# Pooled attention with a noisy top-2 mixture of experts: head sums on another engine, small loads and the first batch in another order

## The chip, the cores and the metric

The kernel runs on one NeuronCore of a Trainium2 chip. The metric is device time in microseconds (us) of one execution. The engines are named as the profile names them: PE (TensorE, matmuls; PEld its weight loads), DVE (VectorE), ACT (ScalarE), POOL (GpSimd), SP (SyncE, which here issues most DMAs). Each engine works through its own queue in order, and an engine that waits holds up everything behind it in that queue.

## What is computed

```
k_p = k.reshape(B, H, S/8, 8, D).mean(3);  v_p likewise      # B=8, H=8, S=576, D=64
scores = q @ k_p^T / sqrt(D);  attn = softmax(scores);  x = attn @ v_p   # x: 4608 tokens x 512
noisy = x @ w_gate + log1p(exp(x @ w_noise)) * noise          # 8 experts
top2, weights = softmax over the two largest of noisy
out = sum over the token's 2 experts of weight * (relu(x @ w1[e]) @ w2[e])   # 512 -> 1024 -> 512
```

## The kernel before, in words

**Attention.** The eight batches are taken as four pairs (`pr` 0 to 3). A pair has five units: two of 256 tokens for each batch and one ("R") that holds the last 64 tokens of both. A unit's tokens are worked on in chunks of 128, so a pair has 9 chunks (`ci` 0 to 8) and the whole attention 36. `k_prep` and `v_prep` add up groups of eight rows of k and v on DVE. `qtr` turns a unit's q on PE (tile `qp`) and ACT copies it out (`qT`). `qk` makes scores on PE (`s`), their maximum on DVE (`mx`) and the exponentials on ACT (`ex`). `et` turns these (`ep`, `eT`), and `av` multiplies them with the block matrix `vbd`. Besides v, `vbd` holds for each head the products of v with that head's rows of the gate and noise weights (`wrb`, multiplied in the step `vr`), so `av` gives the attention output `xr` and, for each of the 8 heads, that head's part of the 16 router logits: `lg`.

**Routing.** `route(pr, ...)` is a generator that runs once per pair. It adds the 8 heads' parts of `lg` (the head sums: for 8 chunks together adds over 128x512, 128x256 and 128x128 elements, then the same for the last chunk over 64, 32 and 16), computes the noisy logits and the two best experts (DVE, four steps on ACT), ranks the tokens by a running count on PE (`rk`, from the mask `mb`), and hands over 18 scatters per pair (`rec_dram`, one DMA each from POOL's queue). The scatters wait in the list `scq` and are issued a few at a time by `advance`, none where `quiet` is 0. Behind them stand, in the same queue, the load of the records of the first expert's rows and the gathers of those rows (`fetch`, tile `xg`).

```
for a, b in ((c0, c1 - 1), (c1 - 1, c1)):
    for h in (4, 2):
        nc.gpsimd.tensor_add(lg[:, a:b, :h], lg[:, a:b, :h], lg[:, a:b, h:2 * h])
    nc.gpsimd.tensor_add(L[:, a - c0:b - c0], lg[:, a:b, 0], lg[:, a:b, 1])
```

**Experts.** Each of the 8 experts takes its rows in three groups: `stage1` multiplies with w1 (8 blocks `f`, line 1016), ACT and DVE split the result into two parts (`hh`, `hl`), and `stage2` multiplies with w2 (lines 1093 and 1127). Expert 0's groups need rows that the four pairs bring in turn: tokens of pairs 0 and 1 for the first group, pair 2 for the second, pair 3 for the third. The last group of each expert (`joined`) comes in three widths; a branch on the expert's row count picks one. The counts are read into PE registers by `count(e)`, which a scheduler places. Pair 3's `rk` matmuls stand on PE behind the first 48 matmuls of `stage1` (4 of the 8 blocks of the first group).

**Order.** Within a priority order that a scheduler keeps, the program's own order decides; `issue_after(x)` holds an instruction behind x. At the start SP issues, in this order: k of batch 0 (three DMAs), q of batch 0 (two), `qr` (the last 64 tokens of q), v of batch 0 (three), and then in `mid_consts` four small DMAs that bring the gate and noise weights turned and doubled, in runs of 8 numbers:

```
for dup in range(2):
    for i, w in enumerate((moe_w_gate, moe_w_noise)):
        nc.sync.dma_start(wr[dup * 64:dup * 64 + 64, :, i * E:(i + 1) * E],
                          w.rearrange("(h d) e -> d h e", d=D))
```

After them POOL copies `wr` into `wrb` (six copies), and SP goes on with k, q, `qr` and v of batch 1.

Of the kernel before, what the change touches and what calls it, by code (L numbers as in the profile page):

```python
# [19 lines left out]
def kernel(  # L20
# [164 lines left out]

    def mid_consts():
        wr = cp.tile([P, H, 2 * E], F32, name="wr")
        for dup in range(2):
            for i, w in enumerate((moe_w_gate, moe_w_noise)):
                nc.sync.dma_start(wr[dup * 64:dup * 64 + 64, :, i * E:(i + 1) * E],  # L190
                                  w.rearrange("(h d) e -> d h e", d=D))
        nc.gpsimd.memset(wrb, 0.0)
        for n in range(NEB):
            rs = slice((n % 2) * 64, (n % 2) * 64 + 64)
            ns = len(HEADS[n])
            nc.gpsimd.tensor_copy(wrb[rs, SLOT0[n]:SLOT0[n] + ns, :],
                                  wr[rs, HEADS[n][0]:HEADS[n][0] + ns, :])

    KT, VT, QT, QR = {}, {}, {}, {}
    lastl, lasta = [None], [None]  # L200

# [77 lines left out]
    def v_prep(b):  # L279
        vt = VT[b]  # L280
        vs = ap_.tile([P, NEB, D], F32, tag="vs", name=f"vs{b}")
        VS[b] = vs
        if PV >> b & 1:
            halves(vt, b, BST, ((0, 3), (3, 6)), PV)
            yield
        yield from pooled(vs[:BST], vt, b, 0, NEB, BST, DV | PV)

# [46 lines left out]
    def qtr(u, half, hp=None):  # L334
# [7 lines left out]
        for i in range(4):  # L342
            if kind == "R":
                src = QR[pr][:, 2 * i:2 * i + 2]
            else:
                src = QT[b][:, half * 4 + i, 2 * jp:2 * jp + 2]
            nc.tensor.transpose(qp[:, i], src.rearrange("p a d -> p (a d)"), ident)  # L347
        with tc.high_priority(offset=HP if hp is None else hp):
            nc.scalar.copy(qT[:, half * 4:half * 4 + 4], qp)

    def qk(u, g):
# [19 lines left out]
        else:  # L371
            s = ps2.tile([P, 512], F32, tag="s", name=f"s{nm}", bufs=SB)
            rows = [(jj, h) for h in GRP[g] for jj in range(2)]
            for i, h in enumerate(GRP[g]):
                nc.tensor.matmul(s[:, i * 2 * G:(i + 1) * 2 * G], qT[:, h], kbd[b % 2][:, h],  # L375
                                 start=True, stop=True)
        n = len(rows)
        sv = s[:, :n * G].rearrange("p (r g) -> p r g", g=G)
        mx = ap_.tile([P, 6], F32, tag="mx", name=f"mx{nm}", bufs=4)
        nc.vector.tensor_reduce(out=mx[:, :n], in_=sv, axis=AX, op=OP.max, negate=True)  # L380
        for i, (jj, h) in enumerate(rows):
# [112 lines left out]
    def route(pr, c0, c1, lg, psum):  # L494
# [10 lines left out]
        L = t(NCH, 2 * E)  # L505
        for a, b in ((c0, c1 - 1), (c1 - 1, c1)):
            for h in (4, 2):
                nc.gpsimd.tensor_add(lg[:, a:b, :h], lg[:, a:b, :h], lg[:, a:b, h:2 * h])  # L508
            nc.gpsimd.tensor_add(L[:, a - c0:b - c0], lg[:, a:b, 0], lg[:, a:b, 1])
            if b < c1:  # L510
# [53 lines left out]
        mb = rp.tile([P, NCH + 1, E], BF16, tag="mb", name=f"mb{pr}_{c0}")  # L564
        nc.gpsimd.memset(mb[:, n:], 0.0)
        V.tensor_add(mb[:, :n], ms[0], ms[1])
# [245 lines left out]
    if WU:  # L812
        wu = ps2.tile([P, 512], F32, tag="s", name="wu", bufs=SB)
        for i in range(WU):
            nc.tensor.transpose(wu[:, i % 4 * P:(i % 4 + 1) * P], ident, ident)
    load_q(0)
    load_qr(0)
    load_v(0)
    block_tiles()
    mid_consts()  # L820
    drain(k_prep(0))
# [36 lines left out]
    qtr(units[0], 0)  # L858
    qtr(units[0], 1)
    for g in range(3):  # L860
        qk(units[0], g)
    if ST & 1:
        qtr(units[1], 0, H0)
        qtr(units[1], 1, H0)
    drain(v_prep(0))
    if ST & 2:
# [8 lines left out]
    for i, (ui, u, jj) in enumerate(chunks):  # L875
# [9 lines left out]
        eT = None  # L885
        quiet = 0 if ci == 0 or ci == NCH - 1 and pr < NP - 1 else 1

# [288 lines left out]
    for i, g in enumerate(groups):  # L1176
# [3 lines left out]
        if joined(g):  # L1180
            count(e)
        stage1(g, (lambda f: hook1(i, f)) if i < 2 else flush if i == len(groups) - 1 else None)
# [131 lines left out]
```

## Time and profile before

| | us |
|---|---|
| runs (3) | 1023.31, 1026.31, 1027.18; median 1026.31 |
| the profiled execution | 1026.68 |
| its span on the core | 1024.9 |
| lies around the span | 1.78 |
| PE busy (share of the span) | 989.9 (97%) |
| DVE, POOL, ACT busy | 546.1, 377.5, 343.8 |

Attention takes the first 190 us or so, the experts the rest. Times in the profile count from the span's start. "Idle before" is how long an engine stood still ahead of an instruction, with what ended the wait behind the arrow. PEclk is the granted share of TensorE's full clock; 1.00 is 2.4 GHz and 0.50 is 1.2 GHz.

### The profile page before, as it was taken

To read this page: it belongs to the slowest core of one execution; us is meant where nothing else is said; L and a number is where in the kernel's file an instruction comes from. 1 tells how busy PE (TensorE), PEld (TensorE's weight loads), DVE (VectorE), ACT (ScalarE), POOL (GpSimd) and SP (SyncE) were. 2 spreads that over 40 slices of the span, in tenths; PEclk is the share of its full clock that TensorE was granted. 3 is DMA by queue.
4 is the path that set the end of the run, shared out by engine and by line. 5 is a ranking of instruction groups with operands and counts; after the bars stand their busy time and mean duration, and the time that the engine had idled before them with its cause. 6 is when DMAs were issued, how large, how long until landed. Compare 5 with 4: busy or idle time off the path is not lost.

```text
span 1024.9 us, 16467 instructions
## 1 busy us (share of the span) xinstructions
PE 989.9 (97%) x5832; PEld 888.6 (87%) x5832; DVE 546.1 (53%) x1261; ACT 343.8 (34%) x857; POOL 377.5 (37%) x433
## 2 busy tenths in 40 slices
PE   7999997979999999999999999999999999999996
PEld 6898896869998888898988898989888988898995
DVE  5799886583344454644464446444644455356341
ACT  4787785451213212411142124211421232123120
POOL 3023574846300442145115421551154215422514
PEclk8999998989999999999999999999999999999998
DMA  9989883344607765676267736772678358744623
GB/s 252 250 250 273 227 263 112 115 146 98 208 15 218 215 180 148 199 238 206 74 188 219 239 114 201 249 217 70 182 235 256 93 161 256 245 144 135 211 87 136
DMA packets 136006, 187.61 MB, mean 183 GB/s; under 512 B 29123, under 2 KB 84052, under 8 KB 135898
## 3 DMA queue, kind: packets, MB, share of 16 engines
q1 hardware_dynamic: 110458, 119.09, 40.5%
q0 software_dynamic: 25440, 67.05, 21.0%
q8 instruction: 72, 1.18, 0.5%
q14 instruction: 36, 0.29, 0.1%
HBM read 123.31 MB, written 70.74 MB: 189 GB/s over the span
## 4 chain that ended last, share of the span: by engine, by line
PE 87%; POOL 3%; issue 3%; ACT 2%; DMA 2%; DVE 1%; SPq 1%; POOLq 0%; ACTq 0%; DVEq 0%
PE bank L1016 37%; PE bank L1127 28%; PE bank L1093 10%; PE a L408 4%; PE s L375 2%; PE ep L393 2%; POOL rec_dram L637 1%; PE qp L347 1%; DMA v<-in_v_dram 1%; ACT ex L382 1%; ACT eT L395 1%; POOL lg L508 1%; POOL out_dram L1072 1%; PE s L365 1%; DMA rec_dram<-rec,pos 0%
## 5 line engine op out<-in xcount | busy, mean ns | idle before, releaser
L1016 PE MATMUL bank<-xh,w 128*128 128x512 f32 (+6 forms) x1536 | 391.2, 339 | 0.0
L1016 PEld LDWEIGHTS bank<-xh,w 128*128 128x128 f32 x1536 | 271.1, 189 | 20.6
L1127 PE MATMUL bank<-w,hh 128*128 128x512 f32 x880 | 271.3, 389 | 0.0
L1016 PE MATMUL bank<-xl,w 128*128 128x512 f32 (+6 forms) x768 | 260.3, 339 | 0.0
L1027 ACT ACTIVATE hh<-bank 128x512 fp32r<-128x512 f32 (+4 forms) x192 | 97.3, 508 | 460.0 <-PE bank L1016 435.7
L1028 DVE SCALAR_TENSOR_TENSOR hl<-bank,hh 128x512 fp32r<-128x512 f32 (+4 forms) x192 | 111.0, 579 | 242.2 <-ACT hh L1027 242.2
L1127 PEld LDWEIGHTS bank<-w,hh 128*128 128x128 f32 x880 | 164.9, 188 | 33.8
L1127 PE MATMUL bank<-w,hl 128*128 128x512 f32 x440 | 171.4, 389 | 0.0
L1016 PEld LDWEIGHTS bank<-xl,w 128*128 128x128 f32 x768 | 145.0, 189 | 10.4
L1064 DVE SCALAR_TENSOR_TENSOR pv<-bank,raw,pv 128x128 f32<-128x128 f32 x196 | 55.5, 342 | 109.1 <-PE bank L1127 62.4
L1068 POOL DMA_DIRECT2D slot_dram<-yt x17 | 9.8, 575 | 270.4 <-DVE yt L1064 218.4
L1093 PE MATMUL bank<-hh,w 128*128 128x240 f32 (+3 forms) x512 | 103.3, 298 | 3.1 <-ACT xh L766 1.8
L1127 PEld LDWEIGHTS bank<-w,hl 128*128 128x128 f32 x440 | 82.6, 188 | 17.2
L637 POOL DMA_INDIRECT rec_dram<-rec,pos x72 | 78.3, 1088 | 48.8 <-issue 14.2
L1048 POOL DMA_INDIRECT pv<-slot_dram,raw x70 | 68.1, 973 | 65.4 <-DMA slot_dram<-ys 33.3
L481 DVE TENSOR_TENSOR w<-wst,w 128x512 fp32r<-128x512 f32 x128 | 82.6, 681 | 10.5 <-ACT w L480 10.5
L1093 PEld LDWEIGHTS bank<-hh,w 128*128 128x128 f32 x512 | 82.5, 189 | 3.6 <-ACT xh L766 2.0
L480 ACT CAST w<-wst 128x512 fp32r<-128x512 f32 x128 | 72.8, 619 | 25.4 <-DMA wst<-in_moe_w_dram 25.2
L714 POOL DMA_INDIRECT row<-x_dram,raw x70 | 70.4, 1006 | 21.4 <-issue 19.8
L1068 POOL DMA_DIRECT2D slot_dram<-pv x55 | 31.7, 577 | 123.8 <-DVE pv L1064 97.1
L1093 PE MATMUL bank<-hl,w 128*128 128x320 f32 (+3 forms) x256 | 75.8, 296 | 0.0
L382 ACT ACTIVATE ex<-s,mx 128x72 f32<-128x72 f32 x288 | 70.6, 344 | 9.9 <-DVE mx L380 9.6
(162 smaller groups left out, 1029.6 us busy)
## 6 DMA issues: line engine op xcount, KB each, us to landing
wst<-in_moe_w_dram SPq DMA_DIRECT2D x64, 512.0 KB
via<-row SPq DMA_DIRECT2D x266, 64.0 KB
xg<-via SPq DMA_DIRECT2D x63, 256.0 KB
slot_dram<-pv POOLq DMA_DIRECT2D x55, 256.0 KB, 4.0
x_dram<-xr SPq DMA_DIRECT2D x16, 512.0 KB
q<-in_q_dram SPq DMA_DIRECT2D x7, 1024.0 KB
k<-in_k_dram SPq DMA_DIRECT2D x6, 896.0 KB
v<-in_v_dram SPq DMA_DIRECT2D x12, 432.0 KB
```

What stands on the lines that cost most here:

```text
L382: lasta[0] = nc.scalar.activation(ex[:, jj, EPOS[h] * G:(EPOS[h] + 1) * G], sv[:, i], AF.Exp, bias=mx[:, i:i + 1])
L480: nc.scalar.copy(hv, sv)
L481: nc.vector.tensor_sub(lv, sv, hv.bitcast(F32))
L637: s = nc.gpsimd.indirect_dma_start(out=rec_dram[:, :], out_offset=bass.IndirectOffsetOnAxis(ap=pos[:, i, c:c + 1], axis=0), in_=rec[:, c, ...
L714: turn_of("pool", lambda: nc.gpsimd.indirect_dma_start(out=row[:32 * nr], out_offset=None, in_=x_dram[:, :], in_offset=bass.IndirectOffset ...
L1016: nc.tensor.matmul(part(ph), w1s(e, a, db, f), part(xs[b][:, db]), start=(i == 0), stop=(i == 3 * NDB - 1))
L1027: act = nc.scalar.activation(hh[:, :n], ph[:, :n], AF.Relu)
L1028: last = nc.vector.scalar_tensor_tensor(hl[:, :n], ph[:, :n], 0.0, hh[:, :n].bitcast(F32), op0=OP.max, op1=OP.subtract)
L1048: turn_of("pool", lambda: nc.gpsimd.indirect_dma_start(out=pv[:np_], out_offset=None, in_=slot_dram[:P + e * CAP, :], in_offset=bass.Indir ...
L1064: nc.vector.scalar_tensor_tensor(r_, y_, wc, pv[:plain] if plain else r_, op0=OP.mult, op1=OP.add)
L1093: nc.tensor.matmul(part(py), w2s(e, b, f)[:, mb * P:(mb + 1) * P], part(hs[f][a]), start=(i == 0), stop=(i == 3 * NFB - 1))
L1127: mm = nc.tensor.matmul(py, hs[f][a][:, cs], w2s(e, b, f), start=(i == 0), stop=(i == 3 * NFB - 1))
```

## The change

- In `route`, the head sums of pairs 2 and 3 run on DVE instead of POOL (12 adds in all); pairs 0 and 1 stay on POOL. The memset of `mb`'s last column moves to DVE for all pairs.
- `quiet` lets scatters through in two more chunks: the last of pair 2 and the first of pair 3.
- The gate and noise weights are loaded as they lie (four DMAs of 8 rows of 2 KB, `mid_loads`, into buffers of the weight ring), turned by 16 small matmuls on PE (tile `wps`) and copied by ACT into `wr`; `qr` of batch 0 is issued after v of batch 0 and these loads instead of before.
- `v_prep` of batch 0 works in three parts, one for each of the three DMAs of v.
- The first unit's scores of heads 0 to 2 stand ahead of the turning of its second half of q; v's preparation stands behind the second score maximum.
- `count(e)` is held behind the last matmul of the group before, for each expert.

```diff
+    def mid_loads():
+        wt = [wp.tile([P, 2 * D * E], F32, tag="wst", name=f"wt{i}", bufs=WS) for i in range(2)]
+        for t, w in zip(wt, (moe_w_gate, moe_w_noise)):
+            for u in range(2):
+                nc.sync.dma_start(t[:H, u * D * E:(u + 1) * D * E], w.rearrange("(h d) e -> h (d e)", d=D))
+        nc.gpsimd.memset(wrb, 0.0)
+        return wt
-    def mid_consts():
+    def mid_consts(wt):
         wr = cp.tile([P, H, 2 * E], F32, name="wr")
-        for dup in range(2):
-            for i, w in enumerate((moe_w_gate, moe_w_noise)):
-                nc.sync.dma_start(wr[dup * 64:dup * 64 + 64, :, i * E:(i + 1) * E],
-                                  w.rearrange("(h d) e -> d h e", d=D))
-        nc.gpsimd.memset(wrb, 0.0)
+        wp_ = ps2.tile([P, 512], F32, tag="one", name="wps", bufs=2)
+        wv = wp_[:, :2 * E * H].rearrange("p (c h) -> p c h", h=H)
+        for i in range(2):
+            src = wt[i][:H].rearrange("h (d e) -> h e d", e=E)
+            for e in range(E):
+                nc.tensor.transpose(wv[:, i * E + e], src[:, e], ident[:H, :H])
+        nc.scalar.copy(wr, wv.rearrange("p c h -> p h c"))
...
-        yield from pooled(vs[:BST], vt, b, 0, NEB, BST, DV | PV)
+        for n0, n1 in ((0, 2), (2, 4), (4, 6)) if b == 0 else ((0, NEB),):
+            yield from pooled(vs[:BST, n0:n1], vt, b, n0, n1, BST, DV | PV)
...
         for a, b in ((c0, c1 - 1), (c1 - 1, c1)):
+            eng = nc.gpsimd if pr < NP // 2 else V
             for h in (4, 2):
-                nc.gpsimd.tensor_add(lg[:, a:b, :h], lg[:, a:b, :h], lg[:, a:b, h:2 * h])
-            nc.gpsimd.tensor_add(L[:, a - c0:b - c0], lg[:, a:b, 0], lg[:, a:b, 1])
+                eng.tensor_add(lg[:, a:b, :h], lg[:, a:b, :h], lg[:, a:b, h:2 * h])
+            eng.tensor_add(L[:, a - c0:b - c0], lg[:, a:b, 0], lg[:, a:b, 1])
...
-        nc.gpsimd.memset(mb[:, n:], 0.0)
+        V.memset(mb[:, n:], 0.0)
...
     load_q(0)
+    load_v(0)
+    wt = mid_loads()
     load_qr(0)
-    load_v(0)
     block_tiles()
-    mid_consts()
...
     qtr(units[0], 0)
-    qtr(units[0], 1)
-    for g in range(3):
-        qk(units[0], g)
-    if ST & 1:
-        qtr(units[1], 0, H0)
-        qtr(units[1], 1, H0)
-    drain(v_prep(0))
+    qk(units[0], 0)
+    with tc.issue_after(lastqk[0].ins):
+        qtr(units[0], 1)
+    qk(units[0], 1)
+    mx1 = lastmx[0]
+    qk(units[0], 2)
+    qtr(units[1], 0, H0)
+    qtr(units[1], 1, H0)
+    with tc.issue_after(lastqk[0].ins):
+        mid_consts(wt)
+    with tc.issue_after(mx1.ins):
+        drain(v_prep(0))
...
-        quiet = 0 if ci == 0 or ci == NCH - 1 and pr < NP - 1 else 1
+        quiet = 0 if ci == 0 and pr <= NP // 2 or ci == NCH - 1 and pr < NP // 2 else 1
...
         if joined(g):
-            count(e)
+            with tc.issue_after(lastmm[0].ins):
+                count(e)
```

Where the order of instructions moves, three places matter.

DVE at the end of pair 2 (`lg` of pair 2; `rt_0_1` is the sum over heads, and line 516, 528 in the changed kernel, is the first step that reads it; `v` and `vs` belong to a batch of pair 3). Before:

```order
L380 TENSOR_REDUCE mx_6_1_0_2139<-s_6_1_0_2135 128x6
L233 TENSOR_TENSOR v_194<-v_194 112x6x256
L414 TENSOR_SCALAR rd_5_1_1_2165<-a_5_1_1_2158 128x8
L380 TENSOR_REDUCE mx_6_1_1_2182<-s_6_1_1_2178 128x6
L415 RECIPROCAL rd_5_1_1_2165<-rd_5_1_1_2165 128x8
L233 TENSOR_TENSOR v_194<-v_194 112x6x128
L419 TENSOR_TENSOR xr_5_1_0_2114<-a_5_1_1_2158,rd_5_1_1_2165 128x512
L421 TENSOR_TENSOR lg_1478<-a_5_1_1_2158,rd_5_1_1_2165 128x128
L380 TENSOR_REDUCE mx_6_1_2_2216<-s_6_1_2_2213 128x4
L414 TENSOR_SCALAR rd_6_0_0_2241<-a_6_0_0_2234 128x8
L516 SCALAR_TENSOR_TENSOR rt_0_2_2203<-rt_0_1_2129 128x72
```

In the changed kernel:

```order
L520 TENSOR_TENSOR lg_1504<-lg_1504 128x8x64
L425 TENSOR_SCALAR rd_5_1_1_2203<-a_5_1_1_2196 128x8
L520 TENSOR_TENSOR lg_1504<-lg_1504 128x8x32
L426 RECIPROCAL rd_5_1_1_2203<-rd_5_1_1_2203 128x8
L521 TENSOR_TENSOR rt_0_1_2156<-lg_1504 128x128
...
L520 TENSOR_TENSOR lg_1504<-lg_1504 128x64
L391 TENSOR_REDUCE mx_6_1_2_2254<-s_6_1_2_2251 128x4
L520 TENSOR_TENSOR lg_1504<-lg_1504 128x32
L425 TENSOR_SCALAR rd_6_0_0_2278<-a_6_0_0_2271 128x8
L521 TENSOR_TENSOR rt_0_1_2156<-lg_1504 128x16
L243 TENSOR_TENSOR v_189<-v_189 112x6x128
L528 SCALAR_TENSOR_TENSOR rt_0_2_2241<-rt_0_1_2156 128x72
```

The six adds stand in DVE's own queue, three before and three after the last chunk's `lg`, and the two adds of `v` have moved behind the first of them; on POOL the 18 scatters of pair 1 now stand in one row with no head sums among them.

DVE at the end of pair 3 (`xl` is a part of the first expert group's rows, which `stage1` reads). Before:

```order
L766 TENSOR_TENSOR xl_0_2666<-xp_2715,xh_0_2665 128x4x128
L766 TENSOR_TENSOR xl_0_2666<-xp_2722,xh_0_2665 128x4x128
L414 TENSOR_SCALAR rd_7_1_1_2740<-a_7_1_1_2733 128x8
L415 RECIPROCAL rd_7_1_1_2740<-rd_7_1_1_2740 128x8
L419 TENSOR_TENSOR xr_7_1_0_2708<-a_7_1_1_2733,rd_7_1_1_2740 128x512
L421 TENSOR_TENSOR lg_2133<-a_7_1_1_2733,rd_7_1_1_2740 128x128
L516 SCALAR_TENSOR_TENSOR rt_0_2_2787<-rt_0_1_2711 128x72
```

In the changed kernel:

```order
L520 TENSOR_TENSOR lg_2163<-lg_2163 128x8x64
L778 TENSOR_TENSOR xl_0_2692<-xp_2748,xh_0_2691 128x4x128
L520 TENSOR_TENSOR lg_2163<-lg_2163 128x8x32
L425 TENSOR_SCALAR rd_7_1_1_2766<-a_7_1_1_2759 128x8
L521 TENSOR_TENSOR rt_0_1_2737<-lg_2163 128x128
L426 RECIPROCAL rd_7_1_1_2766<-rd_7_1_1_2766 128x8
L430 TENSOR_TENSOR xr_7_1_0_2734<-a_7_1_1_2759,rd_7_1_1_2766 128x512
L432 TENSOR_TENSOR lg_2163<-a_7_1_1_2759,rd_7_1_1_2766 128x128
L520 TENSOR_TENSOR lg_2163<-lg_2163 128x64
L520 TENSOR_TENSOR lg_2163<-lg_2163 128x32
L521 TENSOR_TENSOR rt_0_1_2737<-lg_2163 128x16
L528 SCALAR_TENSOR_TENSOR rt_0_2_2813<-rt_0_1_2737 128x72
```

One `xl` stands behind the first big add, and the step that reads the sums follows them directly; further on, one more `hl` add of `stage1` (line 1028, 128x512) stands ahead of `mb`.

PE at the start, after k has been turned. Before:

```order
L347 MATMUL qp_0_0_0_211<-ident,q_150 128x128 x4
L347 MATMUL qp_0_0_1_217<-ident,q_150 128x128 x4
L375 MATMUL s_0_0_0_224<-kbd_159,qT_0_0_210 128x144 x3
L375 MATMUL s_0_0_1_236<-kbd_159,qT_0_0_210 128x144 x3
L347 MATMUL qp_0_1_0_258<-ident,q_150 128x128 x4
L347 MATMUL qp_0_1_1_264<-ident,q_150 128x128 x4
L375 MATMUL s_0_0_2_248<-kbd_159,qT_0_0_210 128x144 x2
L375 MATMUL s_0_1_0_284<-kbd_159,qT_0_1_257 128x144 x3
L317 MATMUL vTp_276<-ident,vs_270 128x112 x3
```

In the changed kernel:

```order
L358 MATMUL qp_0_0_0_206<-ident,q_150 128x128 x4
L386 MATMUL s_0_0_0_213<-kbd_166,qT_0_0_205 128x144 x3
L358 MATMUL qp_0_0_1_225<-ident,q_150 128x128 x4
L386 MATMUL s_0_0_1_231<-kbd_166,qT_0_0_205 128x144
L358 MATMUL qp_0_1_0_253<-ident,q_150 128x128 x4
L386 MATMUL s_0_0_1_231<-kbd_166,qT_0_0_205 128x144 x2
L358 MATMUL qp_0_1_1_259<-ident,q_150 128x128 x4
L201 MATMUL wps<-ident,wt_157 128x8 x8
L201 MATMUL wps<-ident,wt_158 128x8 x8
L386 MATMUL s_0_0_2_243<-kbd_166,qT_0_0_205 128x144 x2
L386 MATMUL s_0_1_0_310<-kbd_166,qT_0_1_252 128x144 x2
L328 MATMUL vTp_302<-ident,vs_290 128x112 x2
```

The first scores stand before the second half's turning, and the 16 small matmuls on the weights stand ahead of the third score group, so PE's queue waits there for the weights' loads.

## Rows read from the trace of the kernel before

**Rows 1.** The page's head.

```profile
span 1024.9 us, 16467 instructions
```

**Rows 2.** Stretches: length, busy us of PE, PEld, DVE, ACT, POOL, PEclk, DMA share, GB/s.

```profile
140.00:151.70 11.70, 11.70 (x98) 11.28 (x97) 10.47 (x22) 10.39 (x37) 9.34 (x8) 1.00 0.86 258
153.40:159.28 5.88, 0.00 (x1) 0.00 (x1) 1.16 (x4) 0.89 (x6) 4.15 (x7) 0.74 0.17 53
159.28:166.40 7.12, 7.12 (x38) 6.07 (x39) 4.05 (x16) 3.59 (x13) 3.36 (x4) 0.50 0.03 3
192.25:203.40 11.15, 11.15 (x51) 8.94 (x49) 1.44 (x5) 0.00 (x0) 9.25 (x12) 1.00 0.30 97
203.40:210.36 6.96, 0.03 (x2) 0.04 (x2) 5.16 (x24) 2.64 (x9) 3.25 (x7) 0.79 0.00 0
210.36:214.20 3.84, 3.84 (x18) 3.16 (x19) 3.84 (x11) 2.63 (x6) 0.54 (x2) 0.50 0.19 30
305.00:983.40 678.40, 676.56 (x3699) 606.78 (x3698) 333.84 (x631) 175.38 (x330) 238.17 (x262) 1.00 0.62 187
```

**Rows 3.** Timeline, end of pair 2: start, us, engine, line, operation, [idle before <-releaser].

```profile
153.60 0.97 POOL L637 DMA_INDIRECT rec_dram<-rec,pos  x1 [0.30 <-issue]
154.59 2.06 POOL L508 TENSOR_TENSOR lg<-lg 128x512 f32<-128x512 f32 x2
158.12 0.23 DVE L516 SCALAR_TENSOR_TENSOR rt<-rt 128x72 f32<-128x72 f32 x1 [6.46 <-POOL rt L509]
159.28 1.21 PE L365 MATMUL s<-kbd,qT 64*64 64x72 f32 x14 [5.91 <-ACT ex L382]
```

**Rows 4.** Timeline, end of pair 3 and the first expert group.

```profile
193.57 0.28 DVE L421 TENSOR_TENSOR lg<-a,rd 128x128 f32<-128x128 f32 x1
203.80 0.23 DVE L516 SCALAR_TENSOR_TENSOR rt<-rt 128x72 f32<-128x72 f32 x1 [9.96 <-POOL rt L509]
210.36 0.23 PE L593 MATMUL bank<-mb,before 128*128 128x80 bf16 x1 [6.93 <-DVE mb L566]
```

**Rows 5.** Timeline, DVE: two-operand adds by size.

```profile
162.39 0.22 DVE L535 TENSOR_TENSOR rt<-rt,rt 128x72 f32<-128x72 f32 x1
162.53 0.68 DVE L481 TENSOR_TENSOR w<-wst,w 128x512 fp32r<-128x512 f32 x1
7.54 0.42 DVE L239 TENSOR_TENSOR ks<-k 128x256 f32<-128x256 f32 x1
```

**Rows 6.** Timeline, the start.

```profile
11.74 2.32 SPq L190 DMA_DIRECT2D wr<-in_moe_w_noise_dram  x1
17.88 2.79 DVE L233 TENSOR_TENSOR v<-v 112x1536 f32<-112x1536 f32 x2 [1.83 <-DMA v<-in_v_dram]
18.39 3.22 POOL L196 COPY wrb<-wr 64x32 f32<-64x32 f32 x6 [11.53 <-DMA wr<-in_moe_w_noise_dram]
24.53 1.19 PE L325 MATMUL vr<-wrb,vT 128*112 128x64 f32 x6
26.81 1.67 PE L408 MATMUL a<-vbd,eT 112*128 112x162 f32 x12
```

**Rows 7.** Timeline, PE, third group of expert 0: into its first and second stage.

```profile
270.52 0.33 PE L1016 MATMUL bank<-xh,w 128*128 128x372 f32 x1
288.38 0.58 PE L1093 MATMUL bank<-hh,w 128*128 128x372 f32 x2 [1.28 <-DVE hl L1028]
```

**Rows 8.** Timeline: one DVE add with POOL idle, one under a scatter.

```profile
33.46 1.75 DVE L233 TENSOR_TENSOR v<-v 112x1536 f32<-112x1536 f32 x1
146.22 1.75 DVE L233 TENSOR_TENSOR v<-v 112x1536 f32<-112x1536 f32 x1
147.05 1.75 POOL L637 DMA_INDIRECT rec_dram<-rec,pos  x1 [0.30 <-DMA rec_dram<-rec,pos]
```

**Rows 9.** Timeline: the last gather of expert 0's third group.

```profile
254.43 0.95 POOL L705 DMA_INDIRECT xg<-x_dram,raw  x1 [0.30 <-issue]
```

**Rows 10.** Chain of waits: start, us, what.

```profile
263.27 1.92 PE bank L755 x16
```

More of the change, by code (lines that the diff above doesn't have):

```diff
@@ L199 @@
     KT, VT, QT, QR = {}, {}, {}, {}
-    lastl, lasta = [None], [None]
+    lastl, lasta, lastqk, lastmx = [None], [None], [None], [None]
     DK, DV = 0, 0
@@ L346, in qtr @@
                 src = QT[b][:, half * 4 + i, 2 * jp:2 * jp + 2]
-            nc.tensor.transpose(qp[:, i], src.rearrange("p a d -> p (a d)"), ident)
+            lastqk[0] = nc.tensor.transpose(qp[:, i], src.rearrange("p a d -> p (a d)"), ident)
         with tc.high_priority(offset=HP if hp is None else hp):
@@ L374, in qk @@
             for i, h in enumerate(GRP[g]):
-                nc.tensor.matmul(s[:, i * 2 * G:(i + 1) * 2 * G], qT[:, h], kbd[b % 2][:, h],
-                                 start=True, stop=True)
+                lastqk[0] = nc.tensor.matmul(s[:, i * 2 * G:(i + 1) * 2 * G], qT[:, h], kbd[b % 2][:, h],
+                                             start=True, stop=True)
         n = len(rows)
@@ L379, in qk @@
         mx = ap_.tile([P, 6], F32, tag="mx", name=f"mx{nm}", bufs=4)
-        nc.vector.tensor_reduce(out=mx[:, :n], in_=sv, axis=AX, op=OP.max, negate=True)
+        lastmx[0] = nc.vector.tensor_reduce(out=mx[:, :n], in_=sv, axis=AX, op=OP.max, negate=True)
         for i, (jj, h) in enumerate(rows):
```

## The prediction

> **What bounds the kernel now.** I read the page's head first, for the length [rows 1]; then the table of stretches, to see in which of them PE, the engine with most work, is not at work or not at its full clock [rows 2]; then, for those stretches, the timeline, where the mark behind a row says how long the engine stood and on whom [rows 3, 4, 6, 7]; last the chain of waits, for what comes next when a wait goes [rows 10].
>
> The reader is to see this. From 305 to 983 us PE is busy 676.56 of 678.40 us at full clock [rows 2]: the experts are PE's work and nothing else, so whatever comes earlier ahead of them makes the whole run shorter by as much. Ahead of them there are two holes. At the end of pair 2 PE does nothing for 5.88 us and then works 7.12 us at PEclk 0.50, the 1.2 GHz level [rows 2]. DVE had stood 6.46 us, and what let it go is POOL's head sum [rows 3]: POOL was still issuing scatters of pair 1, 0.97 us and a 0.30 us pause each, and came to the sums after them. DVE's step held the queue on which the next maxima stand, ACT waited for them, and PE for ACT (5.91 us). At the end of pair 3 the same happens: DVE stands 9.96 us for POOL's head sum, and PE, which had finished its 48 matmuls of the first expert group at about 203.4, stands 6.93 us for `mb` [rows 4] and then runs 3.84 us at 0.50 [rows 2]. A smaller hole is at the start (first `av` matmul at 26.81 [rows 6]), and a fourth of 1.28 us lies inside expert 0's third group [rows 7].
>
> **The sum** is made against the profiled execution, 1026.68 us (span 1024.9 and 1.78 around it), 0.37 us above the median of the runs. About 0.5%, 5 us, is what a measurement of this kernel can tell from no change.
>
> *Head sums of pair 2.* Removed: the wait on POOL. If it goes whole, PE wins 5.88 us, and of the 7.12 us at half clock it wins half, 3.56: 9.44 together. Added on DVE: six adds. Sizes 512 and 256 are 0.68 and 0.42 us; 128 lies between 0.42 and the 0.22 us of 72 elements, I take 0.28; the last three (64, 32, 16) are at most 0.22 each, I take 0.18 [rows 5]. That is 0.68 + 0.42 + 0.28 + 3 x 0.18 = 1.92 us. Just ahead of the hole DVE is busy 10.47 of 11.70 us [rows 2], 90%, so it has about a tenth of its time to hide them in, and the adds stand between the maxima that ACT and PE wait for. Between nothing and 1.92 us I take 1.4, nearer the full price since DVE is so full; ends: 9.4 us if all is hidden, 4.0 us if it is not and the half clock's share does not come back because DVE and ACT (90% and 89% busy there) could not have fed a faster PE. **Term: 8.0 us.** The two adds of `v` that move behind the sums feed a batch that is used chunks later, and cost nothing while the prefetch is that far ahead; without it, 2 us once.
>
> *Head sums of pair 3.* Removed: again POOL. What is late next is the chain from the logits to `mb`: in the old run it takes 210.36 - 203.80 = 6.56 us [rows 4]. In the new order it starts when the last `lg` is done (193.57 + 0.28 = 193.85), later by the three big adds ahead of it (0.68 + 0.42 + 0.28 = 1.38) and the three small ones (0.54), and has one more `hl` add of 0.68 in it: 193.85 + 1.38 + 0.54 + 6.56 + 0.68 = 203.0. PE comes to `rk` at 203.4, so the chain is just in time. PE wins 6.96 us and half of 3.84, 1.92; it loses some 0.5 because one `xl`, which its second matmul reads, now stands behind the 0.68 us add. **Term: 8.4 us**; ends 8.9, and 4 if the chain is some 3 us late, with part of the half clock kept.
>
> *POOL.* It loses 12 adds (2.06 us for the two largest of pair 2 [rows 3]) and issues its scatters without them. Pair 2's scatters need `rec`, pair 3's need `rk`, and both come earlier by what DVE and PE win, so the queue moves along. Its last due time is expert 0's third group: the last gather ends at 254.43 + 0.95 = 255.4 [rows 9], and PE turns those rows at 263.27 [rows 10], so 7.9 us are left for the landing. PE comes there some 20 us earlier, POOL's pair 3 scatters some 18 us minus what their pacing holds back. I charge nothing; the other end stands among the rivals. The two more chunks in which scatters may go move POOL's work to an earlier place, and the `mb` memset is a tenth of a us on either engine.
>
> *Start.* Removed: SP's four weight loads in runs of 8 numbers. The last lands when POOL begins its copies, at 18.39; the copies take 3.22 us [rows 6]. SP spends 2.32 us on issuing the last alone [rows 6], and k of batch 1 waits behind it. Now `qr` is behind v (SP had spent 0.74 us there), so I put v's last third at about 17.1 and the weights at 17.5, PE's 16 small matmuls at 1.3 us (between nothing and 16 x 0.20 us, the rate of the six `vr` matmuls at 1.19), ACT's copy behind its exponentials at 0.4, POOL's copies at 3.22: 22.4. From `vr` to the first `av` it is 26.81 - 24.53 = 2.28 us [rows 6], so `av` can begin at 24.7: 2.1 us. Meanwhile v in thirds takes its DVE work, 2.79 us [rows 6], off the way but for the last 0.9. Heads 0 to 2 have their scores about 1 us earlier, which only feeds this. The wait this adds: PE's queue stands at the 16 matmuls until the weights land, with the third score group, its maximum and ACT's last exponentials of the unit behind it. That is covered as long as the weights land with v, since the first `av` needs v's `vr` in any case; each us that they land later is a us lost. **Term: 2.1 us**, ends 0 and 4.
>
> *Counts.* The old run shows no wait at the third group's first matmul, which has one load before it, and 1.28 us before the second stage, where five loads stand on PE [rows 7]. Now each group has one. **Term: 1.3 us**; ends 1.3, and -0.8 if eight single loads cost 0.26 (1.28 / 5) each.
>
> Sum: 8.0 + 8.4 + 2.1 + 1.3 = 19.8. 1026.7 - 19.8 = 1006.9; with the 0.37 us to the median, **1006.5 us**.
>
> **The rule that speaks against it.** A DVE add under a scatter took 1.75 us, the same as one with POOL idle, and the scatter took 1.75 instead of 0.97 [rows 8]: DVE did not wait, POOL did, by 0.78 us. So the 12 adds cost POOL at most some 3.8 us, their own length, which is inside its 7.9. The Trainium skill, "SBUF — State Buffer", section "SBUF: two separate sides", says that DVE and GpSimd share a pair of ports as an exclusive lock that an add of two SBUF operands needs whenever GpSimd reads SBUF, and that the loser blocks for the whole instruction, whichever started first. By that rule DVE may be the loser, which is the first rival; the trace shows one side of it only.
>
> **The rivals.**
> 1. *DVE's adds wait for the scatters they meet.* Each could stand behind one scatter of 0.97 us: 6 x 0.97 = 5.8 us per pair, off pair 2's term, and off pair 3's as well since its chain has no slack: 19.8 - 11.6 = 8.2, so 1018. Against it: rows 8. Chance 0.06.
> 2. *One of the two holes is only half closed:* pair 3's chain is late by 3 us (its slack is 0.4), or DVE at 90% keeps PE waiting after pair 2 and the half clock stays. Either takes 4 to 5 us: 1011 to 1013. For it: DVE's load. Chance 0.18.
> 3. *The gain is handed back at the third group:* POOL does not move with the others, PE turns the rows where they land now, some 3 us behind 255.4, and then has a half clock to pay: 263.3 - 258.4 = 5 us won and 3 lost, about 1024. Against it: POOL's waits for DVE and for landings, which shrink. Chance 0.04.
> 4. *Slower:* at the same place, if the scatters of pairs 2 and 3, which now run beside a fuller DVE, are stretched by 0.78 us each as in rows 8. POOL starts on them some 10 us earlier (the start's and pair 2's terms), so the gathers end at 255.4 - 10 + the stretch, PE turns the rows 3 us later, and the sign changes where that passes 263.3: at 15 us, 19 of the 36 scatters. At 24 of them, 18.7 us, PE is 4 us later than before there and pays about 2 for the half clock; with the counts' 1.3 won, 1031. Against it: the scatter of rows 3 took 0.97, and in rows 2 DVE has time left at the end of pair 3 (1.44 of 11.15 us busy). Chance 0.04.
>
> **How the numbers follow.** Forecast 0.68, rival 2 0.18, rival 1 0.06, rivals 3 and 4 0.04 each. Low end: all terms at their best, 9.4 + 8.9 + 4 + 1.3 = 23.6, so 1003, and 1.5 for the spread of the runs. High end: rival 2 with a start that gives nothing, 1014.5. What is left out is rivals 1, 3 and 4 and a part of rival 2, under 0.2. Faster by over 0.5% takes in the forecast and rivals 2 and 1: 0.92; within 0.5% is rival 3, 0.04; slower is rival 4, 0.04.
>
> **What would show it.** Right: no DVE idle ended by POOL at the two ends of pairs, PEclk 1.00 from 30 us to the end, `rk` behind the 48 matmuls with under 1 us of PE idle, the first `av` at about 24.7, no idle before the third group's second stage, the experts from 305 on unchanged in length and 20 us earlier. Wrong: a PE wait of over 2 us at pair 3's `mb`, at the third group's turning, or at the 16 small matmuls; DVE adds of the sums longer than in rows 5.

## The result, and the profile after

The changed kernel takes **1008.32 us** (median of 4 runs, 1006.9 to 1010.07); the kernel before, beside it, 1026.12 us (4 runs, 1023.31 to 1027.18). The ratio is 0.9832, 95% interval 0.9807 to 0.9857: faster by 17.8 us, or 1.7%. The profiled run took 1008.26 us with a span of 1006.4, 18.5 us under that of [rows 1]. Forecast were 1006.5 us and a range of 1001.5 to 1014.5.

On three of the four later occasions of measurement the kernel before itself took 1043 to 1048 us instead of 1026, so a run is compared only with runs of its own occasion.

The page's head, of the changed kernel, and its row of the granted clock in 40 slices (9 is 90% or more):

```profile
span 1006.4 us, 16502 instructions
...
PEclk9999999999999999999999999999999999999998
```

The table of stretches of the changed kernel, columns as in [rows 2]. The first two lines are the very stretches of rows 2; the third is from pair 3's `rk` to the second stage of the first expert group; the last is the experts' part, which began at 305 before:

```profile
140.00:151.70 11.70, 11.70 (x98) 11.27 (x97) 11.04 (x28) 10.41 (x37) 9.35 (x8) 1.00 0.86 276
153.40:159.28 5.88, 5.68 (x56) 5.24 (x56) 5.10 (x18) 4.73 (x18) 3.10 (x4) 1.00 0.28 91
...
194.90:206.36 11.46, 11.46 (x60) 9.54 (x60) 11.02 (x39) 6.77 (x13) 5.58 (x6) 1.00 0.60 176
286.36:965.30 678.94, 677.21 (x3701) 607.19 (x3701) 334.43 (x631) 175.14 (x330) 240.73 (x262) 1.00 0.61 186
```

From 153.40 to 159.28 PE did nothing before; now it is busy 5.68 of those 5.88 us, and the clock is 1.00 where [rows 2] show 0.74; from 159.28 to 166.40, at 0.50 before, it is 1.00 too. The experts' part is as long as it was, to 0.6 us (678.94 against 678.40).

The timeline of the changed kernel, DVE, POOL and PE at the ends of pairs 2 and 3:

```profile
145.78 0.97 POOL L649 DMA_INDIRECT rec_dram<-rec,pos  x1 [0.30 <-issue]
...
149.60 2.31 POOL L649 DMA_INDIRECT rec_dram<-rec,pos  x1 [0.31 <-DVE mx L391]
...
146.22 0.68 DVE L520 TENSOR_TENSOR lg<-lg 128x512 f32<-128x512 f32 x1
147.21 0.41 DVE L520 TENSOR_TENSOR lg<-lg 128x256 f32<-128x256 f32 x1
147.66 0.29 DVE L521 TENSOR_TENSOR rt<-lg 128x128 f32<-128x128 f32 x1
150.85 0.22 DVE L520 TENSOR_TENSOR lg<-lg 128x64 f32<-128x64 f32 x1
151.35 0.18 DVE L520 TENSOR_TENSOR lg<-lg 128x32 f32<-128x32 f32 x1
151.58 0.17 DVE L521 TENSOR_TENSOR rt<-lg 128x16 f32<-128x16 f32 x1
...
186.47 0.23 DVE L528 SCALAR_TENSOR_TENSOR rt<-rt 128x72 f32<-128x72 f32 x1
193.24 0.27 DVE L578 TENSOR_TENSOR mb<-rt,rt 128x72 bf16<-128x72 f32 x1
...
177.03 1.23 PE L767 MATMUL xp<-ident,xg 128*128 128x128 f32 x8 [0.26 <-ACT eT L406]
184.11 0.50 PE L1033 MATMUL bank<-xl,w 128*128 128x512 f32 x1 [0.38 <-DVE xl L778]
...
194.90 0.21 PE L605 MATMUL bank<-mb,before 128*128 128x80 bf16 x1
```

The step that reads the sums (line 528, once 516) carries no wait; in [rows 3, 4] it stood 6.46 and 9.96 us for POOL. `mb` is done at 193.51, and PE comes to `rk` at 194.9 without standing. A new stall is 0.38 us, at the `xl` that now has one of the adds ahead of it.

How far PE has come shows in the chain of waits (start, us, what). Before, with [rows 10]:

```profile
223.53 10.88 PE bank L1127 x48
...
270.68 16.43 PE bank L1016 x96
287.76 0.63 DVE hl L1028
288.39 16.65 PE bank L1093 x96
305.04 21.80 PE bank L1016 x96
```

In the changed kernel:

```profile
206.36 10.88 PE bank L1144 x48
...
246.10 1.92 PE bank L767 x16
...
253.51 16.42 PE bank L1033 x96
269.93 16.43 PE bank L1110 x96
286.36 21.80 PE bank L1033 x96
```

The lead is 17.17 us at the first group's second stage (223.53 - 206.36), the same 17.17 at the third group's turning and first stage, 18.46 behind its second stage's start, and 18.68 at the end of expert 0. The first `xp` matmul (the turning of the first expert group's gathered rows, during pair 3) stands at 177.03, and in the kernel before at 186.06, so 9.03 us had been won there:

```profile
186.06 1.23 PE L755 MATMUL xp<-ident,xg 128*128 128x128 f32 x8 [0.26 <-ACT eT L395]
```

### The profile page after: what moved, and what is told of

Its sections match the earlier page's. It is cut to its first block, busy times and chain, and to the rows that moved or that the text cites. A ratio compares the mean times of both kernels' runs of the same rounds, so it can differ in the third digit from the quotient of the medians.

```text
span 1006.4 us, 16502 instructions
## 1 busy us (share of the span) xinstructions
PE 986.1 (98%) x5848; PEld 885.0 (88%) x5848; DVE 549.6 (55%) x1283; ACT 344.5 (34%) x858; POOL 373.7 (37%) x417
## 4 chain that ended last, share of the span: by engine, by line
PE 90%; ACT 3%; issue 2%; DVE 1%; POOL 1%; DMA 1%; SPq 0%; POOLq 0%; ACTq 0%; DVEq 0%
PE bank L1033 38%; PE bank L1144 28%; PE bank L1110 10%; PE a L419 4%; PE s L386 3%; PE ep L404 2%; PE qp L358 2%; ACT ex L393 1%; ACT eT L406 1%; POOL out_dram L1089 1%; PE kT L309 0%; PE vr L336 0%; ACT kbd L313 0%; DMA k<-in_k_dram 0%; PE s L376 0%
## 5 line engine op out<-in xcount | busy, mean ns | idle before, releaser
L726 POOL DMA_INDIRECT row<-x_dram,raw x70 | 70.4, 1006 | 21.4 <-issue 19.8
```

The costliest lines, as they stand in the source:

```text
L726: turn_of("pool", lambda: nc.gpsimd.indirect_dma_start(out=row[:32 * nr], out_offset=None, in_=x_dram[:, :], in_offset=bass.IndirectOffset ...
```

## The experiments

The theory: the gain is the two holes, pair 2's worth about 9 us and pair 3's about 8; 1.3 come from the counts and none from the start. The rival: the sums alone are not enough, and a part of the gain is the start's. The first four kernels take the change apart.

**Sums alone** (the kernel before, with pairs 2 and 3 summed on DVE):

```diff
+            eng = nc.gpsimd if pr < NP // 2 else V
             for h in (4, 2):
-                nc.gpsimd.tensor_add(lg[:, a:b, :h], lg[:, a:b, :h], lg[:, a:b, h:2 * h])
+                eng.tensor_add(lg[:, a:b, :h], lg[:, a:b, :h], lg[:, a:b, h:2 * h])
-            nc.gpsimd.tensor_add(L[:, a - c0:b - c0], lg[:, a:b, 0], lg[:, a:b, 1])
+            eng.tensor_add(L[:, a - c0:b - c0], lg[:, a:b, 0], lg[:, a:b, 1])
```

> The kernel before, with the twelve head-sum adds of pairs 2 and 3 on VectorE and nothing else changed (the chunks in which scatters may go, the `mb` memset, the start and the counts are as before). Theory (terms read from the two traces): the adds alone close both holes, 9.0 + 8.1 = 17.1 us, so 1026.1 - 17.1 = 1009.0; no PE idle over 1 us at the ends of pairs 2 and 3, first `av` at 26.8, 1.28 us before the third group's second stage still there. The prediction's own terms give 8.0 + 8.4 = 16.4, 1009.7. Rival: the adds need the two more chunks for POOL's scatters; without them POOL is late at expert 0's third group, PE waits there for 4 us or more, and the time is 1013 or above.

**Pair 2's sums back on POOL** (the changed kernel):

```diff
-            eng = nc.gpsimd if pr < NP // 2 else V
+            eng = nc.gpsimd if pr < 3 else V
```

> The changed kernel with the six adds of pair 2 on POOL again, pair 3's on VectorE. Theory: pair 2's term alone comes back, 9.0 us, 1008.3 + 9.0 = 1017.3, and pair 3's end keeps its 0.4 us of idle. The prediction's term: 8.0, so 1016.3. Rival: the two holes are one debt of POOL's (its scatters run late, and whoever asks POOL last pays); then with pair 2's sums on POOL the hole at pair 2 is smaller or larger than 5.88 us of PE idle by several us, and the time is off 1017 by over 3.

**Pair 3's sums back on POOL** (the changed kernel):

```diff
-            eng = nc.gpsimd if pr < NP // 2 else V
+            eng = nc.gpsimd if pr != 2 else V
```

> The changed kernel with the six adds of pair 3 on POOL again, pair 2's on VectorE. Theory: pair 3's term alone comes back, 8.1 us, 1016.4; DVE stands about 10 us for POOL's sum and PE about 7 for `mb`. The prediction's term: 8.4, so 1016.7. Rival (one debt of POOL's): with pair 2's adds gone and pair 2 done 9 us sooner POOL has more scatters in front of pair 3's sums, and the hole grows by 3 us or more, to 1019.5 or above; or POOL is sooner through, and it shrinks to under 5 us.

**The old start** (the changed kernel; weights by the strided loads, the order of loads and of scores as before, v in one part):

```diff
     load_q(0)
-    load_v(0)
-    wt = mid_loads()
     load_qr(0)
+    load_v(0)
...
+    mid_consts(mid_loads())
...
-        for n0, n1 in ((0, 2), (2, 4), (4, 6)) if b == 0 else ((0, NEB),):
-            yield from pooled(vs[:BST, n0:n1], vt, b, n0, n1, BST, DV | PV)
+        yield from pooled(vs[:BST], vt, b, 0, NEB, BST, DV | PV)
```

> The changed kernel with all of the start as before: strided weight loads and no turning on PE, `qr` ahead of `v`, all scores of the first unit behind both turnings, `v` of batch 0 in one part; head sums, counts and the rest as changed. Theory: the start gave nothing, so 1008.3 with the first `av` at 26.8, and batch 1's kT at 29.1 in both. The prediction's term: 2.1 us longer, 1010.4, with everything behind 34 us later by as much.

Measured, with the kernel before at 1048.19 us (31 runs): 1047.7, 1051.89, 1044.98 and 1044.66 us; ratios 0.9992 (0.9953 to 1.0032), 1.0034 (1.0002 to 1.0067), 0.9974 (0.9943 to 1.0005), 0.9958 (0.9923 to 0.9993). None of the expected times is there: in all of them PE stood at places where neither kernel's record shows a stall, the longest in the first, and as long in the third:

```profile
203.51 2.34 PE L756 MATMUL xp<-ident,xg 128*128 128x128 f32 x8 [7.49 <-issue]
```

"issue" says that PE waited for nothing that the profile shows. The times therefore tell little: only the second (0.3% slower than the kernel before) and the last (0.4% faster) have intervals that leave out 1, the second barely. The waits tell more. With pair 2's sums back on POOL, DVE stands for them at the end of pair 2 and PE behind DVE:

```profile
178.38 0.23 DVE L528 SCALAR_TENSOR_TENSOR rt<-rt 128x72 f32<-128x72 f32 x1 [5.09 <-POOL rt L521]
...
179.74 0.65 PE L404 MATMUL ep<-ident,ex 128*112 128x128 f32 x4 [4.50 <-ACT qT L360]
```

With pair 3's sums back, DVE stands 2.94 us for POOL there (222.22), and PE comes to `rk` at 228.71 without a wait. Where a pair's sums are on DVE, as both are in the first and last kernel, that wait is not there. So the wait goes and comes with the sums, pair by pair. It is not the old order that comes back, though: beside the changed `quiet`, POOL works on the first group's gathers until 177.37 before it turns to pair 2's last three adds, which in the kernel before stand ahead of those gathers.

The question left is whether the unexplained stops belong to the four kernels or to the occasion.

**The two kernels unaltered.** No edit.

> The changed kernel itself, beside the kernel before, as a control: in the experiments so far the kernel before took 1048.2 us instead of 1026.1, and PE stood up to 7.5 us at places where no engine shows a wait, beside runs of POOL's scatters. Theory A (those stops belong to the chip or the time of the run, and take the gain): where the kernel before takes about 1048, the changed one takes 1043 to 1046, with PE idle 25 us or more between 80 and 220 us; where it takes about 1026, the changed one takes 1008. Theory B (the gain of 17.8 us is the same wherever it runs): 17 to 19 us less than the kernel before, whatever that takes.

> The kernel before itself, for a profile beside the others. Theory A: where it takes about 1048, its profile has the same stops of PE beside scatters as the experiments (over 15 us of them between 80 and 220 us) on top of the two holes of 5.9 and 7.0 us; where it takes 1026 it has none of over 2 us. Theory B: only the two holes, and its extra 22 us lie elsewhere.

The changed kernel took 1041.38 us (ratio 0.9991, 0.9956 to 1.0026), the kernel before 1042.84. So it is the occasion. The table of stretches, one line per kernel: before and changed on record, then the same two here.

```profile
80.00:320.00 240.00, 223.57 (x1501) 200.90 (x1500) 149.78 (x460) 116.16 (x350) 112.18 (x121) 0.96 0.56 161
```

```profile
80.00:320.00 240.00, 237.04 (x1583) 212.00 (x1582) 159.28 (x487) 119.99 (x355) 112.34 (x114) 1.00 0.60 175
```

```profile
80.00:320.00 240.00, 212.72 (x1413) 187.99 (x1413) 144.83 (x451) 112.22 (x341) 112.19 (x121) 0.94 0.52 152
```

```profile
80.00:320.00 240.00, 215.74 (x1414) 190.82 (x1414) 147.11 (x466) 112.26 (x339) 105.46 (x106) 0.93 0.50 146
```

In the stretch in which the change works, PE lost 11 and 21 us of busy time to the record, and the two kernels are alike; past 320 us PE is as busy as on record. The timeline of the kernel before on this occasion:

```profile
150.39 1.10 PE L393 MATMUL ep<-ident,ex 128*112 128x128 f32 x4 [3.27 <-issue]
199.47 2.38 PE L755 MATMUL xp<-ident,xg 128*128 128x128 f32 x8 [4.62 <-issue]
...
166.15 0.23 DVE L516 SCALAR_TENSOR_TENSOR rt<-rt 128x72 f32<-128x72 f32 x1 [0.43 <-POOL rt L509]
215.49 0.23 DVE L516 SCALAR_TENSOR_TENSOR rt<-rt 128x72 f32<-128x72 f32 x1 [1.07 <-POOL rt L509]
```

PE stops at 147 and 195 us, while POOL issues scatter after scatter, most of them at the usual 0.97 us. By the time PE, ACT and DVE bring the logits, POOL is nearly through: DVE waits for its sums 0.43 and 1.07 us, not 6.46 and 9.96. Little is left to remove: 1.5 us of waits and, if it is there too, the 1.3 of the counts, against 1.5 us measured between the two, which is inside their intervals. That is the same mechanism from its other side: **the head sums cost only as much as POOL is later than PE's side.**

**The start, two trials.** The trace of the changed kernel shows v's last third late; so v in one part, and in a second kernel the first adds of k of batch 1 on POOL:

```diff
-        for n0, n1 in ((0, 2), (2, 4), (4, 6)) if b == 0 else ((0, NEB),):
-            yield from pooled(vs[:BST, n0:n1], vt, b, n0, n1, BST, DV | PV)
+        yield from pooled(vs[:BST], vt, b, 0, NEB, BST, DV | PV)
```

> The changed kernel with `v` of batch 0 prepared in one part again, the rest of the new start kept. Theory (the third part's turning behind two steps of PE's queue is what holds `vr` back: vTp at 24.15, vT at 25.08, vr at 25.68): vTp is whole about 2 us sooner, `vr` at about 24 and the first `av` at 25 to 26 instead of 27.0; but batch 1's kT stays at 29.0, since it waits for `ks`, which stands in VectorE's queue; so the time does not change (within 0.5 us of the changed kernel in the trace at 34 us). Rival (the first `av` is what sets the start): everything behind it comes 1 to 2 us earlier.

```diff
-    PK, PV = 0, 0
+    PK, PV = 2, 0
```

> The changed kernel with the first adds of `k` of batch 1 (1.49 us on VectorE) on POOL, which is idle from 22 us on. Theory (VectorE's queue up to `ks` of batch 1 is the bound of the start, about 90% busy from 17 to 29 us): `ks` ends about 1 to 1.5 us sooner, kT of batch 1 at about 27.7, and everything behind 34 us is up to 1.5 us earlier. Rival (PE or the loads bound the start): kT stays at 29.0 and nothing moves; or VectorE's other operations stretch beside POOL's adds and the gain is given back.

Measured: 1041.72 us (0.9988, 0.995 to 1.0027) and 1045.71 us (0.9999, 0.9965 to 1.0034; the medians alone would give 1.003), with the kernel before at 1042.59. The places tell more than the times: the first `av` matmuls start at 28.76 and 25.54 (two of them, the other ten at 26.41), those of the second chunk at 35.47 and 33.01, against 27.04 and 33.64 in the changed kernel. Batch 1's `kT`, which the expectations name, starts at 30.82 and 28.43, against 29.06. The first trial's weights were turned 2.3 us later, at 19.63, so it settles nothing about the thirds; the second's 0.63 us lies within what this place differs by between executions (32.62 to 35.24 in the executions of the changed start below). Neither is an improvement that can be shown.

**No scatters** (both kernels; each of the 72 scatters is replaced by a small copy and three memsets on POOL, at the same place and with the same pacing):

```diff
-            s = nc.gpsimd.indirect_dma_start(
-                out=rec_dram[:, :],
...
+            s = nc.gpsimd.tensor_copy(idle.bitcast(I32)[:, :RW], rec[:, c, i, :])
...
+            for _ in range(3):
+                with tc.issue_after(s.ins):
+                    s = nc.gpsimd.memset(idle, 0.0)
+            lasts[0] = s
```

> The kernel before with each of its 72 scatters of records replaced, at the same place of POOL's queue and with the same pacing, by a copy of 4 numbers and three memsets of 384 (about as long as a scatter's 0.97 us and its pause of 0.30); so no records are written, the gathers all read one row, and the output is not the reference's. Theory A (PE's stops of up to 7 us belong to POOL's scatters): no PE stop of over 1 us that no engine's wait explains between 90 and 260 us; the holes at the ends of pairs 2 and 3 are back, DVE standing 4 us or more for POOL's head sums at each; about 1020 to 1030. Rival (the stops come from something else: the clock, PE's own instructions, the transfers): over 10 us of such stops stay, no DVE wait for POOL at the ends of the pairs, about 1035 to 1048.

> The changed kernel with its 72 scatters replaced by a copy and three memsets in the same way; again no records, and the output is not the reference's. Theory A (without the scatters PE does not stop, and what the change removes is POOL's lateness at the ends of two pairs): 14 to 19 us less than the same edit on the kernel before (1003 to 1012), no DVE wait for POOL at the ends of pairs 2 and 3, PE without a stop over 1 us from 90 to 260 us. Rival (stops from something else): within 3 us of the other, about 1035 to 1045.

Measured: 1032.8 us (4 runs, 1029.2 to 1034.16) from the kernel before and 1018.93 us (4 runs, 1017.01 to 1022.45) from the changed one, with the full kernel before at 1045.99 beside them. The stops of PE that nothing explains are gone, on an occasion that has them, and with them gone the change is worth 13.9 us again, a little less than the 14 to 19 expected; both times are above their expected ranges. A stand-in keeps POOL 1.68 us (its copies start at 198.85 and 200.53) where a scatter and its pause take 1.27, so POOL is later here than on record, and the 13.9 us are no measure of the change with undisturbed scatters. The timeline without scatters, kernel before:

```profile
166.12 0.23 DVE L518 SCALAR_TENSOR_TENSOR rt<-rt 128x72 f32<-128x72 f32 x1 [7.02 <-POOL rt L511]
166.87 0.50 PE L365 MATMUL s<-kbd,qT 64*64 64x72 f32 x2 [6.60 <-ACT kbd L302]
...
207.97 0.23 DVE L518 SCALAR_TENSOR_TENSOR rt<-rt 128x72 f32<-128x72 f32 x1 [6.83 <-POOL rt L511]
215.13 0.22 PE L595 MATMUL bank<-mb,before 128*128 128x80 bf16 x1 [4.41 <-POOL idle L645]
```

and the changed kernel without scatters:

```profile
19.37 1.90 PE L201 MATMUL wps<-ident,wt 8*128 8x8 f32 x16 [1.31 <-DMA wt<-in_moe_w_gate_dram]
...
205.14 0.21 PE L607 MATMUL bank<-mb,before 128*128 128x80 bf16 x1
```

Both holes of [rows 3, 4] are back in the one: DVE stands 7.02 and 6.83 us for POOL's sums, and PE 6.60 and 4.41 us behind it. (The mark on PE's last row names a stand-in's memset; `mb`, which the matmul reads, was done by DVE at 214.98, just before it.) Both are closed in the other (a smaller one at pair 1, 3.43 and 3.07 us, is in both; its sums stay on POOL in either kernel). Of the 13.9 us, 10.0 are there at `rk` (215.13 against 205.14), although this execution of the changed kernel starts its second chunk 2.0 us later (35.24 against 33.23). So this pair supports the theory with the scatters out of the way; the 13.9 us are of the whole change, not of the sums alone.

**Gathers for scatters, and half the scatters** (the changed kernel; the first replaces the 72 scatters by gathers of the same size into an unread tile, the second replaces only the 36 of the second choices, by copy and memsets as above):

```diff
-                out=rec_dram[:, :],
-                out_offset=bass.IndirectOffsetOnAxis(ap=pos[:, i, c:c + 1], axis=0),
-                in_=rec[:, c, i, :], in_offset=None)
+                out=sink[:, c * 2 + i, :], out_offset=None, in_=rec_dram[:, :],
+                in_offset=bass.IndirectOffsetOnAxis(ap=pos[:, i, c:c + 1], axis=0))
```

> The changed kernel with each of its 72 scatters replaced by a gather of the same size (128 rows of 16 bytes, the same row numbers, from the records' place in memory into a tile that nothing reads), at the same place of POOL's queue and with the same pacing; so no records are written, and the output is not the reference's. Where the kernel before takes over 1035: Theory D (what stops PE is POOL's making and issuing of an indirect transfer): the stops stay, PE has 15 us or more of unexplained idle time between 90 and 260 us, 1033 or more. Theory W (what stops PE are the scattered writes to memory): no stop over 1 us, and the time is that of the changed kernel without scatters, 1015 to 1023. Where the kernel before takes about 1026, neither has stops, and this run tells nothing of them.

```diff
+            if i == 0:
+                s = nc.gpsimd.indirect_dma_start(
...
+                return
+            s = nc.gpsimd.tensor_copy(idle.bitcast(I32)[:, :RW], rec[:, c, i, :])
```

> The changed kernel with every second scatter (those of the second choices, 36 of 72) replaced by a copy and three memsets as in the kernels without scatters; half of the records are missing, and the output is not the reference's. Where the kernel before takes over 1035: if each scatter adds its share to the stops, PE's unexplained idle time between 90 and 260 us is about half of the changed kernel's and the time about 1030, midway between 1041 and 1019. Rival (the stops need scatters close behind one another): well under half, 1023 or less. Rival (a few scatters are enough to stop PE at its fixed places): nearly all of it stays, 1037 or more.

Measured: 1006.75 us (0.9821, 0.9805 to 0.9838) and 1005.98 us (0.9802, 0.9786 to 0.9818), with the kernel before at 1025.81. On this occasion the kernel before took its time on record, and the traces of these two show no stop, so they don't tell what in a scatter stops PE; that stays open. What they do tell: with the changed schedule but for the scatters, 19.1 and 19.8 us are gained on such an occasion a second time, and gathers in place of scatters, or half as many scatters, make no difference that can be shown (the intervals overlap that of the changed kernel, 0.9807 to 0.9857).

## Why the prediction was right, and where it was not

**Pair 2, 8.0 us: 9.0.** The second chunk's `av` starts at 33.63 and 33.64 us in the two executions on record, and at 145.78 us POOL issues the same scatter in both, so all of the 9.03 us at `xp` is this pair's: 5.88 of hole and the half clock's 3.56 are 9.44, which leaves 0.4 for the adds where the prediction charged 1.4. The adds themselves came as sized: 0.68 + 0.41 + 0.29 + 0.22 + 0.18 + 0.17 = 1.95 us, forecast 1.92. DVE is busy 11.04 of 11.70 us there now (10.47 in [rows 2]) and PE still 11.70: the adds were hidden better than "nearer the full price" has it.

**Pair 3, 8.4 us: 8.1.** 17.17 - 9.03 = 8.14. The last logits are done at 185.74, and `mb` at 193.51: 7.8 us, where the prediction's own working has 203.0 - 193.85 = 9.2. The three big adds, which it put behind the last logits, had already run between 182.72 and 184.71, so the chain was done 1.4 us ahead of `rk` rather than 0.4. The loss at `xl`, put at 0.5, is 0.38.

**Counts, 1.3 us: 1.3.** The lead grows from 17.17 to 18.46 between the third group's first and second stage, 1.29 us; the five loads' stall [rows 7] has no successor, and the chain goes from 253.51 to 286.36 on PE alone. The profile put the old stall down to DVE's last `hl` add. The changed kernel speaks against that, since its second stage starts 0.83 us ahead of the same add:

```profile
269.77 0.51 PE L1110 MATMUL bank<-hh,w 128*128 128x372 f32 x2
270.60 0.62 DVE L1045 SCALAR_TENSOR_TENSOR hl<-bank,hh 128x448 fp32r<-128x448 f32 x1 [1.48 <-ACT hh L1044]
```

That the loads made the wait is so far shown by the two positions only; no run moved the loads alone.

**Start, 2.1 us: 0.** This is the step that failed: "From `vr` to the first `av` it is 26.81 - 24.53 = 2.28 us [rows 6], so `av` can begin at 24.7". The timeline of the changed kernel:

```profile
17.33 1.92 PE L201 MATMUL wps<-ident,wt 8*128 8x8 f32 x16
...
19.95 2.21 POOL L206 COPY wrb<-wr 64x32 f32<-64x32 f32 x6 [13.13 <-ACT wr L202]
...
22.87 0.28 DVE L249 TENSOR_TENSOR vs<-v 112x128 f32<-112x128 f32 x1
24.15 0.39 PE L328 MATMUL vTp<-ident,vs 112*128 112x112 f32 x1
25.08 0.45 ACT L331 COPY vT<-vTp 128x336 f32<-128x336 f32 x1
25.68 0.75 PE L336 MATMUL vr<-wrb,vT 128*112 128x64 f32 x6 [1.13 <-ACT vT L331]
27.04 1.67 PE L419 MATMUL a<-vbd,eT 112*128 112x162 f32 x12
```

and of the kernel before, all of v being turned together:

```profile
22.53 0.44 ACT L320 COPY vT<-vTp 128x336 f32<-128x336 f32 x1 [0.51 <-PE vTp L317]
```

The weights are ready as forecast: `wrb` is done at 22.16, put at 22.4. But `vr` also needs `vT`, and that is no longer first: v's last third leaves DVE at 23.15, stands on PE behind scores until 24.15 and on ACT until 25.53. The prediction took the weights for the only late operand and let `vr` follow them at once; it follows 3.5 us later. They were not late even before: there `wrb` was done at 21.61 [rows 6] and `vT` at 22.97, and `vr` started at 24.53, with no wait marked, behind scores in PE's own queue. The 16 turnings took 1.92 us, between the 1.3 taken and the bound's upper end of 3.2.

From those turnings to the first 12 `av` it is 9.3 to 10.3 us in every one of seven executions with the changed start (9.71 on record; the two trials of the start left out), where the prediction's own working has 24.7 - 17.5 = 7.2. So when the weights land late, `av` is late with them: in the changed kernel without scatters PE waits 1.31 us for them until 19.37 (above), and `av` begins at 28.64. Four of the seven have such a wait, of 0.22 to 1.70 us. That is the added wait that the prediction named, at about the price it gave. The second chunk's `av` start at 32.07 to 34.33 in five executions with the old start (mean 33.3) and at 32.62 to 35.24 in seven with the new (mean 34.0): a gain of nothing, and perhaps a small loss. The part gives nothing in the profile; that it could be left out without loss is not shown by a run without stops.

The first `av` is also not what the rest goes by. In all fourteen executions the second chunk's `av` starts 4.56 to 4.66 us after batch 1's `kT`, which follows DVE's last add of k; on record `kT` is at 29.06 in both kernels, though the first `av` is 0.23 us later in the changed one. What is won or lost at the second chunk does carry on: in the two kernels of the last pair it starts 1.02 us earlier and 1.13 later than in the changed kernel, and pair 2's first add on DVE does so too, by the same amounts (145.20 and 147.35 against 146.22).

**The rule and the rivals.** DVE's adds did not wait for a scatter to end: the add at 146.22 and the scatter at 145.78 overlap by half a microsecond and took 0.68 and 0.97 us, as each does elsewhere; the longest the same add took is 0.73 us, at 182.72 beside a scatter of 0.97. Where one lost, it was again the scatter, 2.31 us at 149.60 beside DVE's work. The lock that the Trainium skill describes ("SBUF — State Buffer", section "SBUF: two separate sides"), by which the one that starts first keeps the shared pair and the other blocks for that whole instruction, cost the sums at most this 0.05 us in the trace; the measurement decides. Rival 1 (1018) did not come. Nor did rival 2: both holes are closed whole, and the clock is 1.00 in every stretch shown. Rivals 3 and 4 are out too: POOL moved along, the last gather of expert 0's third group starts at 237.22 where [rows 9] have 254.43, and PE turns its rows at 246.10 without a wait, 7.9 us behind the gather, as before.

The sum was 19.8 and came to 18.5 in the span: -2.1 for the start, +1.0 for pair 2, -0.3 for pair 3 leave 18.4. That the forecast lies only 1.8 us off is in part luck, since pair 2's surplus covers half of the start's miss. What no experiment measures is what each pair is worth in time: the kernels made for it ran beside stops and show the waits alone, so 9.0 and 8.1 rest on the two executions on record. Nor was the change of `quiet`, or of `mb`'s memset, run without the sums beside an undisturbed kernel.

## What to carry to other kernels

A step moved off a late engine is worth what that engine is late by where the step is waited for, hole and half clock together, and no more; when the bounding engine is itself late, as beside the stops, the same edit is worth next to nothing. Before making an operand earlier, see whether its reader waited for it at all, and how soon the other operand is there: follow both back before taking the old distance between two rows as the new one. And measure the old kernel beside every experiment: without it, most of these runs would have read as a change that fails.

## What was not expected of the hardware

On three of four occasions PE stood up to 7.49 us with no cause in the profile, at much the same places of the program, between 90 and 262 us, where POOL issues scatters and gathers; one and the same chip showed it on two occasions and not on a third (kernel before 1042.59 and 1045.99, then 1025.81 us). In the longest stop of the kernel with the sums alone, ACT and DVE stand too, with a mark that names no engine:

```profile
202.87 0.59 ACT L395 COPY eT<-ep 112x512 f32<-112x512 f32 x1 [7.12 <-remote]
203.56 0.17 DVE L414 TENSOR_SCALAR rd<-a 128x8 f32<-128x8 f32 x1 [8.00 <-remote]
```

Both read what PE had made by 196.03 as the profile has it, while POOL went on with scatters of 0.97 us. As the ends of matmuls are modelled, the rows do not say whether PE's last results came late or the word of them did. The stops were gone when copies and memsets stood in the scatters' place. What a scatter does there is open.
